# Sliding-window attention with a gated feed-forward on one core: inverse softmax sums spread by TensorE transposes of a widened copy, applied one step later

## The chip, the cores and the metric

One core of one Trainium2 chip. The metric is the device time of one execution in microseconds. Each engine works through a queue of its own in order: TensorE (PE, its weight loads shown apart as PEld), VectorE (DVE), ScalarE (ACT), GpSimd (POOL) and the queue that issues most DMAs (SP). An instruction that waits at the head of a queue holds everything behind it.

## What is computed

The reference, cut to what matters:

```python
# attention: B=4, H=8, S=768, D=64, 8 global keys, 96 local keys
scores = (q @ k.T) / 8 + bias          # bias = -slope(head) * distance
scores = where(keep, scores, -1e9)     # keep: key is global, or 0 <= q - k < 96
a = exp(scores - max(scores))
a = a / (sum(a) + 1e-9)                # the inverse sums: one number for each query and head
x = a @ v                              # -> [B, S, 512]
# feed-forward, 512 -> 1024 -> 512
h = relu(x @ w_in)
c = conv over 3 neighbouring positions of h, weights conv_w
out = (h * sigmoid(c)) @ w_out
```

The weights of the feed-forward come as float64 and are decoded on the chip.

## The kernel before, in words

**Work units.** A *job* m is one batch, one half of the sequence (384 queries) and one pair of heads: 32 jobs. A job has three *steps* i = 0, 1, 2 of 128 queries, so there are 96 steps s = 3m + i. Four jobs make one *unit* n, whose 384 positions then go through the feed-forward: 8 units.

**One step.** `scores` (L373) multiplies 128 queries with 232 keys for both heads on TensorE; `maxima` (L408) adds the bias and takes the row extremum on VectorE; `exps` (L425) takes the exponential on ScalarE, whose accumulator gives the row sums, into `sums[m]`. Two steps later (`LAG_T`) `transposes` (L454) turns the exponentials on TensorE into the PSUM tile `t`, four transposes a step, and ScalarE copies them to `pt` (L464, L465, L467).

**One job's end.** `inverses(m)` (L436) takes the reciprocals of the 6 sums of each query row on VectorE, [128 queries, 6]. They are needed the other way round: `pv[m]`, the product with v, has head dimension on partitions (64 for each of two heads) and 384 queries along the row, so that each query's inverse must stand on all 64 partitions of its head. Before, `spread(m)` (L441) transposes [128, 6] to [6, 128] on TensorE (L443), copies that to `row` on ScalarE (L445), and issues six DMAs on SP (L449), each of which repeats one row of 128 numbers over 64 partitions of `rs[m]`. `values(m)` (L470) multiplies v with `pt` into `pv[m]` on TensorE (24 matmuls, L475), and at its end multiplies `pv[m]` with `rs[m]` on VectorE (L486), rounds the product to `xh` on ScalarE (L487) and takes the rest `xl` on GpSimd (L488). `xh` and `xl` are the input of the feed-forward. `spread(m-1)` stands in step (m, 1) and `values(m-1)` in step (m, 2).

**The feed-forward.** `mm1` (L495) forms h with three passes over the four jobs' `xh`, `xl` (L506), `relu` moves it to `hbuf` (L519 on ScalarE, L517 on VectorE), `conv` is one instruction on GpSimd (L555) and two on VectorE (L556, L557), `gate` and `saturated` are on ScalarE (L575, L586), `split` on VectorE, ScalarE and GpSimd (L607 to L610), `mm2` on TensorE (L619). These items stand in a queue, and `fill(k)` puts some of them between the attention's instructions of each step, `k` being what is left divided by `left`, the steps still to go in the unit.

**What sets the order.** In the first 11 steps (`HAND`) the order on all engines is that of the code. From then on only TensorE's order is that of the code; a scheduler orders the other engines by its own model of time. In the first steps TensorE also runs idle multiplications (`warm`, L163). The first five jobs (`NATIVE`) multiply q and k as they are loaded (L389), later ones after a split by `prep` (L134 to L145) into `qh`, `ql`, `kk` (L399). The weights' decoding (L318, L320, L322 on VectorE, L327 on ScalarE, L334 on GpSimd) is put into the steps piece by piece, 16 pieces of 512 KB (loads on SP, L305).

**PSUM.** There are eight banks: three for scores (`ps_s`), one for transposes (`ps_t`), one for `pv` (`ps_v`; the transposed sums stand in the same bank), three for the feed-forward (`ps_m`). A native step takes two banks of `ps_s`, a later step one.

## Time and profile before

| | |
|---|---|
| three runs | 563.7, 564.24, 567.82 us; median 564.24 us |
| the profiled execution's own time | 566.89 us |
| its span, first to last instruction | 565.1 us |
| mean granted TensorE clock | 0.914 of full speed |
| VectorE, ScalarE, GpSimd busy | 373.5, 303.9, 257.9 us |
| DMA | 68.10 MB, mean 121 GB/s |
| rs<-row | 192 DMAs of 32 KB, median 4.6 us from issue to landing |

Lines named L... are those of the kernel before. In a list of waits the columns are the waiting engine and line, the releaser, the total in us, the number of times and the longest. In a timeline they are start, duration in us, engine, line, instruction, and in brackets the engine's idle time before it with its releaser. In a row of one line's instructions, the three numbers behind the count are the shortest, median and longest duration in ns.

The execution has five stretches that the text refers to: set-up and the first steps (0 to 23 us), the rest of the native steps (23 to 73 us), steps in which most of the weights are decoded beside the first unit (73 to 125 us), the regular steps (125 to 500 us), and the end (500 to 565 us), where the last unit's feed-forward runs and the weights are read once more for a check of their range.

### The profile page before, as it was taken

To read this page: it belongs to the slowest core of one execution; us is meant where nothing else is said; L and a number is where in the kernel's file an instruction comes from. 1 tells how busy PE (TensorE), PEld (TensorE's weight loads), DVE (VectorE), ACT (ScalarE), POOL (GpSimd) and SP (SyncE) were. 2 spreads that over 40 slices of the span, in tenths; PEclk is the share of its full clock that TensorE was granted. 3 is DMA by queue.
4 is the path that set the end of the run, shared out by engine and by line. 5 is a ranking of instruction groups with operands and counts; after the bars stand their busy time and mean duration, and the time that the engine had idled before them with its cause. 6 is when DMAs were issued, how large, how long until landed. Compare 5 with 4: busy or idle time off the path is not lost.

```text
span 565.1 us, 9158 instructions
## 1 busy us (share of the span) xinstructions
PE 474.3 (84%) x3045; PEld 405.1 (72%) x3045; DVE 373.5 (66%) x825; ACT 303.9 (54%) x825; POOL 257.9 (46%) x210
## 2 busy tenths in 40 slices
PE   7686686676967899998978899899978899988795
PEld 6464465575965689787867798788867788777584
DVE  5346599996796758754867788557669677137720
ACT  2345475665756556652565646644655487246710
POOL 4023477663873745673554355574534442233000
PEclk8957688887997979998998899999979899999999
DMA  6844876645553644465555654475545534476511
GB/s 193 200 93 106 186 216 181 139 125 127 101 115 22 149 89 96 115 139 117 107 107 108 143 90 81 78 169 127 109 55 129 118 44 78 82 209 197 179 57 43
DMA packets 38328, 68.10 MB, mean 121 GB/s; under 512 B 6145, under 2 KB 19969, under 8 KB 38273
## 3 DMA queue, kind: packets, MB, share of 16 engines
q1 hardware_dynamic: 34816, 61.28, 50.5%
q10 hardware_dynamic: 3456, 6.16, 2.9%
q8 instruction: 26, 0.43, 0.3%
q14 instruction: 30, 0.24, 0.1%
HBM read 54.84 MB, written 6.29 MB: 108 GB/s over the span
## 4 chain that ended last, share of the span: by engine, by line
DMA 22%; DVE 22%; PE 22%; SPq 12%; ACT 11%; issue 8%; POOL 2%; DVEq 0%; ACTq 0%; POOLq 0%
DMA rs<-row 15%; SPq L449 11%; PE h L506 9%; PE o L619 7%; DVE c L557 3%; DMA check<-in_w_in 3%; DVE c L556 3%; ACT pbuf L430 3%; DVE s L418 3%; DVE c L607 2%; DMA check<-in_w_out 2%; DVE rs L486 2%; DVE w L320 2%; ACT sat L586 1%; PE s L399 1%
## 5 line engine op out<-in xcount | busy, mean ns | idle before, releaser
L430 ACT ACTIVATE pbuf<-s,mm 128x232 f32<-128x232 f32 (+1 forms) x192 | 82.1, 433 | 68.5 <-DVE mm L418 66.7
L555 POOL TENSOR_SCALAR c<-hbuf,cw 128x382 f32<-128x382 f32 (+1 forms) x64 | 47.7, 748 | 78.7 <-ACT hbuf L519 41.4
L619 PE MATMUL o<-woh,gh 128*128 128x512 f32 x192 | 82.5, 430 | 0.8 <-ACT hbuf L519 0.7
L418 DVE CUSTOM_DVE_ANT_0 s<-s,tab 128x232 f32<-128x232 f32 (+1 forms) x192 | 73.0, 385 | 15.2 <-PE s L399 8.2
L619 PE MATMUL o<-woh,gl 128*128 128x512 f32 x192 | 78.4, 408 | 2.9 <-DVE gl L610 2.9
L619 PE MATMUL o<-wol,gh 128*128 128x512 f32 x192 | 78.4, 408 | 0.0
L506 PE MATMUL h<-xh,wih 128*128 128x384 f32 x252 | 60.3, 358 | 18.6 <-ACT xh L487 15.0
L460 PE MATMUL t<-ident,pbuf 128*128 128x128 f32 (+1 forms) x192 | 55.6, 311 | 23.7 <-ACT pt L467 17.2
L488 POOL TENSOR_TENSOR xl<-rs,xh 128x384 fp32r<-128x384 f32 x32 | 37.8, 1180 | 81.0 <-ACT xh L487 74.8
L145 POOL TENSOR_TENSOR ql<-rq,qh 128x768 fp32r<-128x768 f32 x24 | 48.3, 2011 | 44.3 <-DVE qh L140 23.8
L143 POOL TENSOR_TENSOR kk<-rk,kk 64x1008 fp32r<-64x1008 f32 (+1 forms) x27 | 61.0, 2260 | 11.8 <-POOL ql L145 4.5
L556 DVE SCALAR_TENSOR_TENSOR c<-hbuf,cw,c 128x382 f32<-128x382 f32 (+1 forms) x64 | 52.0, 815 | 19.6 <-POOL c L555 19.3
L506 PE MATMUL h<-xl,wih 128*128 128x384 f32 x252 | 62.0, 370 | 0.2 <-POOL xl L488 0.2
L506 PEld LDWEIGHTS h<-xh,wih 128*128 128x128 f32 x252 | 45.9, 199 | 22.1 <-ACT xh L487 17.1
L506 PE MATMUL h<-xh,wil 128*128 128x384 f32 x252 | 61.4, 369 | 0.0
L467 ACT ACTIVATE pt<-t 128x512 f32<-128x512 f32 x80 | 47.1, 589 | 22.0 <-PE t L461 22.0
L475 PE MATMUL pv<-pt,v 104*64 104x128 f32 (+2 forms) x768 | 55.1, 289 | 2.4 <-ACT row L445 1.5
L557 DVE SCALAR_TENSOR_TENSOR c<-hbuf,cw,c 128x382 f32<-128x382 f32 (+1 forms) x64 | 54.9, 858 | 0.8
L460 PEld LDWEIGHTS t<-ident,pbuf 128*128 128x128 f32 (+1 forms) x192 | 27.7, 144 | 38.5 <-ACT pt L467 21.3
L475 PEld LDWEIGHTS pv<-pt,v 104*64 104x64 f32 (+2 forms) x768 | 43.4, 141 | 15.1 <-issue 6.2
L486 DVE TENSOR_TENSOR rs<-pv,rs 128x384 f32<-128x384 f32 x32 | 17.7, 553 | 54.6 <-DMA rs<-row 50.8
L461 PE MATMUL t<-ident,pbuf 128*128 128x128 f32 x192 | 53.2, 299 | 0.0
(112 smaller groups left out, 990.4 us busy)
## 6 DMA issues: line engine op xcount, KB each, us to landing
v<-in_vv SPq DMA_DIRECT2D x32, 384.0 KB, 4.2
rq<-in_qk SPq DMA_DIRECT2D x27, 384.0 KB, 4.0
rk<-in_qk SPq DMA_DIRECT2D x15, 504.0 KB, 3.6
rs<-row SPq DMA_DIRECT2D x192, 32.0 KB, 4.6
out<-ob ACTq DMA_DIRECT2D x23, 256.0 KB, 2.1
rk<-in_qk SPq DMA_DIRECT2D x12, 408.0 KB, 3.8
wr<-in_w_in SPq DMA_DIRECT2D x8, 512.0 KB, 5.5
wr<-in_w_out SPq DMA_DIRECT2D x8, 512.0 KB, 4.4
```

Source lines behind the costliest of these rows:

```text
L143: G.tensor_tensor(kk[64:], rk[64:], kk[64:].bitcast(F32), ALU.subtract)
L145: X.tensor_tensor(ql, rq, qh.bitcast(F32), ALU.subtract)
L418: last_ttr[s] = V.tensor_tensor_reduce(out=sp[j][:, c0 : c0 + n], in0=sp[j][:, c0 : c0 + n], in1=tb, scale=-0.125, scalar=3.0e38, op0=ALU. ...
L430: last_exp[s] = A.activation(pb[:, j, c0 : c0 + n], sp[j][:, c0 : c0 + n], AF.Exp, bias=mm[:, j : j + 1], scale=-1.0, accum_out=sums[m][:, ...
L449: nc.sync.dma_start(rs[m][64 * j : 64 * j + 64, i * P : (i + 1) * P], row[c : c + 1].unsqueeze(1).broadcast_to([1, D, P]),)
L460: T.transpose(pt[:ka, j, 0, :], pb[:, j, c0:P], ident)
L461: T.transpose(pt[:, j, 1, :], pb[:, j, P:256], ident)
L475: T.matmul(pv[m][64 * j : 64 * j + 64, i * P : (i + 1) * P], vt[m][:n, i, c, 64 * j : 64 * j + 64], sb[:n, j, c, :], start=c == 0, stop=c ...
L506: T.matmul(ps[:, :TB], w_[:, k, fs], x_, start=part == 0 and k == 0, stop=part == 2 and k == NK - 1,)
L556: V.scalar_tensor_tensor(c, *tap(0), c, ALU.mult, ALU.add)
L557: V.scalar_tensor_tensor(c, *tap(2), c, ALU.mult, ALU.add)
L619: T.matmul(ps, g_[:, f], w_[:, f], start=f == 0 and part == 0, stop=f == NF - 1 and part == 2,)
```

## The change

The six DMAs, the transposition to [6, 128] and the copy to `row` are gone. Instead `spread(m)` widens the inverses on GpSimd: each of a query's 6 numbers is repeated 64 times, giving `wide`, [128, 3 x 128]. It now stands directly behind `inverses(m)`, in step (m+1, 0). A new function `turned(m)`, directly behind `values(m)`, transposes the three 128 x 128 blocks of `wide` on TensorE into a bank of `ps_t`, and ScalarE copies the 384 columns to `rs[m]`. The product with `pv`, `xh` and `xl` become a function of their own, `mixed(m)`, one step after `values(m)`; since the feed-forward's input is complete a step later, a unit's queue is spread over one step more (`left`).

With the sums' transposition gone from it, `pv[m]` is allocated in `values`. `ps_s` has two banks and `ps_t` two; native steps take their second head's scores from `ps_m`. `sums` is laid out by step and head. `load_v(m)` is issued in step (m, 0), behind the values of job m-2 that free its buffer, instead of a step earlier; the native loads go one job further ahead (job 2 gets buffers of its own and is loaded in step 1). `rs` and `wide` have one buffer each, where `rs` had two.

```diff
-    ps_s = pool("ps_s", 3, space=PSUM)
-    ps_t = pool("ps_t", 1, space=PSUM)
+    ps_s = pool("ps_s", 2, space=PSUM)
+    ps_t = pool("ps_t", 2, space=PSUM)
...
-            rk = p2.tile([P, w // 2], F32, tag="kk", name=f"rk{m}")
-            rq = p2.tile([P, TB], F32, tag="qh", name=f"rq{m}")
+            rk = (p1 if m == 2 else p2).tile([P, w // 2], F32, tag="rk" if m == 2 else "kk", name=f"rk{m}")
+            rq = p2.tile([P, TB], F32, tag="ql" if m == 2 else "qh", name=f"rq{m}")
...
-            sp = [ps_s.tile([P, 256], F32, tag="s", name=f"s{s}_{j}") for j in range(2)]
+            other = ps_m.tile([P, 512], F32, tag="m", name=f"s{s}_1")
+            sp = [ps_s.tile([P, 256], F32, tag="s", name=f"s{s}_0"), other]
...
     def spread(m):
-        pv[m] = ps_v.tile([P, TB + P], F32, tag="v", name=f"pv{m}")
-        T.transpose(pv[m][: 2 * NB, TB:], sums.pop(m)[:, 2], ident)
-        row = p1.tile([2 * NB, P], F32, tag="row", name=f"row{m}")
-        A.activation(row, pv[m][: 2 * NB, TB:], AF.Copy)
-        rs[m] = p2.tile([P, TB], F32, tag="rs", name=f"rs{m}")
-        for c in range(2 * NB):
-            j, i = divmod(c, NB)
-            nc.sync.dma_start(
-                rs[m][64 * j : 64 * j + 64, i * P : (i + 1) * P],
-                row[c : c + 1].unsqueeze(1).broadcast_to([1, D, P]),
-            )
+        inv = sums.pop(m)[:, 2]
+        wide = p2.tile([P, NB, 2, D], F32, tag="wide", name=f"wide{m}", bufs=1)
+        G.tensor_copy(wide, inv.unsqueeze(3).broadcast_to([P, NB, 2, D]))
+        wides[m] = wide.rearrange("p i j d -> p i (j d)")
+
+    def turned(m):
+        wide = wides.pop(m)
+        pt = ps_t.tile([P, 2, 2, P], F32, tag="t", name=f"rt{m}")
+        flat = pt.rearrange("p j c q -> p (j c q)")[:, :TB]
+        for i in range(NB):
+            T.transpose(flat[:, i * P : (i + 1) * P], wide[:, i], ident)
+        rs[m] = p2.tile([P, TB], F32, tag="rs", name=f"rs{m}", bufs=1)
+        A.activation(rs[m], flat, AF.Copy)
...
     def values(m):
+        pv[m] = ps_v.tile([P, TB], F32, tag="v", name=f"pv{m}")
...
+    def mixed(m):
         xh = px.tile([P, TB], F32R, tag="xh", name=f"xh{m}")
...
             if ends(s - LAG_V):
                 values((s - LAG_V) // NB)
+                turned((s - LAG_V) // NB)
             if s >= LAG_T:
                 transposes(s - LAG_T)
             maxima(s)
             exps(s)
+            if ends(s - LAG_V - 1):
+                mixed((s - LAG_V - 1) // NB)
             if i == 0 and m:
                 inverses(m - 1)
-            elif i == 1 and m:
                 spread(m - 1)
...
-                left = SPU - (e + 1) % SPU
+                left = SPU - (e + 1) % SPU + 1
                 if e + 1 >= len(steps) - SPU:
-                    left += 2
+                    left += 1
...
+            if ends(e):
+                mixed(e // NB)
             if s <= len(steps) and i < 1:
                 inverses((s - 1) // NB)
-            elif s == len(steps) + 1 or i == 1:
-                spread(s // NB - 1)
+                spread((s - 1) // NB)
...
+        elif s == 1:
+            load(2)
...
-            if 1 <= m < NATIVE - 1:
-                load(m + 1)
+            if 1 <= m < NATIVE - 2:
+                load(m + 2)
...
-        if s >= 2 and (s - 2 - (LAG_V - 3)) % NB == 0:
-            load_v((s - 2 - (LAG_V - 3)) // NB + 1)
+        if s >= NB and i == 0:
+            load_v(m)
```

**VectorE at the first job's end, before.** L486 is job 0's product; the first ISA rows behind it are step 5's maxima, then come a limit check and a weight piece's decoding (`w`).

```order
L322 SCALAR_TENSOR_TENSOR w_0_284<-wr_0_214,w_0_284 128x512
L486 TENSOR_TENSOR rs_353<-pv_349,rs_353 128x384
L418 ISA s_0_382,mm_411<-s_0_382,tab 128x232
L418 ISA mm_411 128x1
L418 ISA s_1_383,mm_411<-s_1_383,tab 128x232
L418 ISA mm_411 128x1
L236 TENSOR_SCALAR misc<-num 128x1
```

The same place in the changed kernel, where the product is L492:

```order
L322 SCALAR_TENSOR_TENSOR w_0_290<-wr_0_214,w_0_290 128x512
L419 ISA s_0_380,mm_410<-s_0_380,tab 128x232
...
L318 TENSOR_SCALAR w_0_429<-wr_0_252 128x512
L320 SCALAR_TENSOR_TENSOR w_0_429<-wr_0_252,w_0_429 128x512
L419 ISA s_0_433,mm_443<-s_0_433,tab 128x136
L419 ISA mm_443 128x1
L419 ISA s_1_432,mm_443<-s_1_432,tab 128x136
L419 ISA mm_443 128x1
L492 TENSOR_TENSOR rs_400<-pv_383,rs_400 128x384
```

The product has moved behind the maxima of steps 5 and 6 and two decoding instructions of the next weight piece.

**TensorE at the start of a unit's feed-forward (unit 3, steps 51 and 52), before.** `o` is the previous unit's second product, `s` the scores of step 51, `h_0` the first block of the new unit; `xh_2617` is the input that the last job gives.

```order
L619 MATMUL o_5_2563<-wol,gh_5_1980 128x512
L619 MATMUL o_5_2563<-woh,gl_5_1981 128x512
L399 MATMUL s_2644<-kk_2537,qh_2535 128x136
L399 MATMUL s_2644<-kk_2537,ql_2536 128x136
L399 MATMUL s_2644<-kk_2537,qh_2535 128x136
L399 MATMUL s_2644<-kk_2537,ql_2536 128x136
L506 MATMUL h_0_2657<-xh_2137,wih 128x384
L506 MATMUL h_0_2657<-xh_2316,wih 128x384
L506 MATMUL h_0_2657<-xh_2480,wih 128x384
L506 MATMUL h_0_2657<-xh_2617,wih 128x384
```

In the changed kernel (`xh_2601` is the last job's; the first `s` row is step 51's, the second step 52's; what is left out holds four transposes and ten further `o` rows):

```order
L400 MATMUL s_2590<-kk_2492,ql_2491 128x136
L625 MATMUL o_5_2545<-woh,gh_5_1978 128x512
...
L625 MATMUL o_5_2545<-woh,gl_5_1979 128x512
L400 MATMUL s_2641<-kk_2492,qh_2490 128x232
...
L512 MATMUL h_0_2651<-xh_2129,wih 128x384
L512 MATMUL h_0_2651<-xh_2309,wih 128x384
L512 MATMUL h_0_2651<-xh_2461,wih 128x384
L512 MATMUL h_0_2651<-xh_2601,wih 128x384
```

Twelve matmuls of the unit before, four transposes and step 52's scores now stand between step 51's scores and the first use of the last job's `xh`.

More of the change, by code (lines that the diff above doesn't have):

```diff
@@ L370, in fast_path @@
     last_ttr = {}
-    st_s, st_pt, pv, xt, sums, rs, line = {}, {}, {}, {}, {}, {}, {}
+    st_s, st_pt, pv, xt, sums, rs, wides = {}, {}, {}, {}, {}, {}, {}
     def scores(s):
@@ L413, in maxima @@
         if i == 0:
-            sums[m] = p1.tile([P, 3, 2 * NB], F32, tag="sums", name=f"sums{m}", bufs=3)
+            sums[m] = p1.tile([P, 3, NB, 2], F32, tag="sums", name=f"sums{m}", bufs=3)
         for j in range(2):
@@ L431, in exps @@
                 pb[:, j, c0 : c0 + n], sp[j][:, c0 : c0 + n], AF.Exp,
-                bias=mm[:, j : j + 1], scale=-1.0, accum_out=sums[m][:, 0, NB * j + i : NB * j + i + 1],
+                bias=mm[:, j : j + 1], scale=-1.0, accum_out=sums[m][:, 0, i, j : j + 1],
             )
@@ L485, in values @@
         x = rs.pop(m)
-        V.tensor_tensor(x, pv[m][:, :TB], x, ALU.mult)
+        V.tensor_tensor(x, pv[m], x, ALU.mult)
         cur["mixed"] = A.activation(xh, x, AF.Copy)
@@ L811, in fast_path @@
                 values((s - LAG_V) // NB)
+                turned((s - LAG_V) // NB)
             if s < len(steps) + LAG_T:
```

## Prediction

> **What bounds the kernel now.** First the page, for shares and the chain that ended last:
>
> ```profile
> span 565.1 us, 9158 instructions
> PE 474.3 (84%) x3045; PEld 405.1 (72%) x3045; DVE 373.5 (66%) x825; ACT 303.9 (54%) x825; POOL 257.9 (46%) x210
> DMA 22%; DVE 22%; PE 22%; SPq 12%; ACT 11%; issue 8%; POOL 2%; DVEq 0%; ACTq 0%; POOLq 0%
> ```
>
> No engine is full. TensorE is nearest, and a third of the chain is DMAs and the queue that issues them. What binds differs by stretch, so next the busy time by window:
>
> ```profile
> core 0: us, PE busy (x) PEld busy (x) DVE busy (x) ACT busy (x) POOL busy (x), PEclk, DMA share, GB/s
> 0.00:23.00 23.00, 18.86 (x178) 15.11 (x178) 12.23 (x45) 8.36 (x28) 7.09 (x30) 0.93 0.72 206
> 23.00:73.00 50.00, 32.70 (x179) 23.02 (x179) 26.62 (x74) 20.85 (x67) 16.49 (x14) 0.69 0.62 133
> 73.00:125.00 52.00, 36.94 (x241) 33.27 (x242) 51.00 (x92) 33.66 (x87) 37.08 (x25) 0.87 0.63 166
> 125.00:500.00 375.00, 334.35 (x2223) 291.76 (x2222) 255.05 (x547) 214.82 (x586) 191.23 (x134) 0.94 0.52 104
> 500.00:565.00 65.00, 51.49 (x229) 41.90 (x227) 28.57 (x67) 26.21 (x59) 6.02 (x8) 0.96 0.44 137
> ```
>
> From 23 to 73 us nothing is full: something waits. From 73 to 125 us VectorE is (51.0 of 52). From 125 to 500 us TensorE works 334.35 of 375 us; it stands 40.65 us. So the third view is the waits: VectorE's in the first 125 us and TensorE's from 125 to 500 us, the largest of each.
>
> ```profile
> DVE rs L486 <- DMA rs<-row: 22.9, 5, 9.0
> ...
> PE h L506 <- ACT xh L487: 15.0, 7, 3.4
> PE t L460 <- ACT pt L467: 10.7, 7, 3.4
> PE pv L443 <- DVE sums L439: 8.1, 1, 8.1
> PE t L460 <- ACT pt L465: 6.3, 5, 1.6
> ```
>
> The first row is VectorE standing for the spread inverses. The next four add up to 40.1 us, nearly all that TensorE stands in the regular steps. How one wait spreads shows in the timeline at 44 us, one row each of VectorE, ScalarE and TensorE:
>
> ```profile
> 44.40 0.56 DVE L486 TENSOR_TENSOR rs<-pv,rs 128x384 f32<-128x384 f32 x1 [9.02 <-DMA rs<-row]
> ...
> 44.99 0.52 ACT L487 ACTIVATE xh<-rs 128x384 fp32r<-128x384 f32 x1 [7.94 <-DVE rs L486]
> ...
> 46.52 0.82 PE L389 MATMUL s<-rk,rq 64*128 64x136 f32 x2 [4.65 <-ACT pbuf L430]
> ```
>
> The product stands at the head of VectorE's queue for 9.02 us with the next maxima behind it; ScalarE stands 7.94 us, and TensorE waits for exponentials that waited for those maxima.
>
> **The change, part by part. Product behind the DMAs, 0 to 125 us.** The DMAs go, and the product moves a step back, behind two steps' maxima; its `rs` then comes from TensorE and ScalarE. At most the 22.9 us vanish. But from 23 to 73 us 50 x 133 = 6650 KB of loads must still come, at the 206 GB/s of the first stretch 32 us, so no more than 18 of the 50 us can go (VectorE's 26.62 us of work allow more). I hold that at least one longest stall, 9 us, goes. The value taken is 16, nearer the upper end since loads have nothing of the DMA's waits ahead of them on SP any more. The native steps' other edits (second head's scores in another pool, earlier loads, `load_v` later) serve these same steps and are counted in the 16.
>
> **Widening on GpSimd.** 32 copies of 128x384, not seen before. The nearest rows are the one-input instruction of about that size and the two-input one of exactly that size; behind them two VectorE lines, 32-bit decoding and the cast of `kk`:
>
> ```profile
> L555 POOL TENSOR_SCALAR c<-hbuf,cw x64: 584/594/1409, 80.2 to 524.7; 128x382 f32<-128x382 f32 x32, 128x386 f32<-128x386 f32 x32
> L488 POOL TENSOR_TENSOR xl<-rs,xh x32: 995/1017/2002, 28.8 to 494.8; 128x384 fp32r<-128x384 f32 x32
> ...
> L320 DVE SCALAR_TENSOR_TENSOR w<-wr,w x16: 651/693/2848, 12.7 to 113.9; 128x512 int32<-128x512 int32 x16
> ...
> L136 DVE CAST kk<-rk x19: 656/2264/2420, 180.5 to 449.9; 128x1008 fp32r<-128x1008 f32 x11, 128x816 fp32r<-128x816 f32 x8
> ```
>
> I take 0.59 us a copy (bounds 0.58 and 1.02), 19 us in all, which fits into GpSimd's idle half; were that cover gone, all 19 us would show. But equal VectorE instructions differ fourfold, the median cast 2.26 us against 0.66 at best: they seem to be held up while GpSimd works. Where VectorE is full, 73 to 125 us, some five copies fall: between 0 and 5 x 0.59 = 3 us. I take +1, the middle being 1.5 and a copy often meeting an instruction that is not held.
>
> The Trainium skill speaks against the change here ("SBUF — State Buffer", section "SBUF: two separate sides"): GpSimd and VectorE share a pair of ports under an exclusive lock, held for a whole instruction, and a GpSimd instruction that reads SBUF blocks a VectorE one with two SBUF inputs. The two VectorE rows above agree with it. By that rule the full 3 us would be lost in that stretch, and the sum would stand 2 us higher.
>
> **Transposes on TensorE.** Three a job in place of one; their pace and the small one's are seen at 290 and 292 us:
>
> ```profile
> 290.27 0.27 PE L461 MATMUL t<-ident,pbuf 128*128 128x128 f32 x1
> 290.37 0.27 PE L460 MATMUL t<-ident,pbuf 128*128 128x128 f32 x1
> 290.48 0.27 PE L461 MATMUL t<-ident,pbuf 128*128 128x128 f32 x1
> ...
> 292.31 0.27 PE L399 MATMUL s<-kk,ql 128*128 128x232 f32 x1
> 292.42 0.27 PE L443 MATMUL pv<-ident,sums 128*6 128x128 f32 x1
> 296.09 0.33 PE L460 MATMUL t<-ident,pbuf 128*128 128x128 f32 x1 [3.40 <-ACT pt L467]
> ...
> 298.14 0.63 PE L619 MATMUL o<-woh,gl 128*128 128x512 f32 x1
> 298.56 0.63 PE L619 MATMUL o<-woh,gh 128*128 128x512 f32 x1
> 298.99 0.63 PE L619 MATMUL o<-wol,gh 128*128 128x512 f32 x1
> ```
>
> One starts 0.11 us after another, the small one 0.11 after its forerunner. From 125 us on 24 jobs end: 24 x 3 x 0.11 = 7.9 us come, 24 x 0.11 = 2.6 go. TensorE is the fullest engine there, so the whole +5.3 counts (bounds 0, if they lie in its waits, and 7.9).
>
> **ScalarE.** A copy of 384 columns out of PSUM (the row of `hbuf`, of that size and source) in place of `row`:
>
> ```profile
> L519 ACT ACTIVATE hbuf<-h x50: 462/488/507, 77.8 to 524.2; 128x384 f32<-128x384 f32 x50
> ...
> L445 ACT ACTIVATE row<-pv x32: 248/250/267, 19.3 to 485.4; 6x128 f32<-6x128 f32 x32
> ```
>
> 24 x (0.488 - 0.250) = 5.7 us more beside 214.82 of 375: hidden under TensorE's work, at worst 5.7.
>
> **TensorE's waits, 125 to 500 us.** Of the 8.1 us for VectorE's reciprocals I count 5: TensorE meets the widened sums one step later, behind `values`, and the 375 us hold some 70 steps of 5 us. The 15.0 for `xh` should go too: as the order rows show, twelve matmuls, four transposes and four scores now lie between, and the product no longer waits for a DMA. Of the 17.0 for `pt` I count half, 8: with two banks two transposes in a row are free, but `turned` takes one of them, so that the transposes behind `values` still need the eviction of the step before, and the next ones that of `rs`. That is 28. A part comes back as waits for whatever is then late: VectorE's 255.05 us in a shorter stretch, ScalarE's in-order queue. I take four fifths, 22 (bounds 10, the reciprocals' 5 and a third of the `xh` waits, and 40).
>
> The clock is a second gain. Behind the 3.40 us gap above, `o` matmuls start 0.43 us apart; 291 us shows the usual pace:
>
> ```profile
> 291.29 0.39 PE L619 MATMUL o<-woh,gh 128*128 128x512 f32 x1
> 291.52 0.39 PE L619 MATMUL o<-wol,gh 128*128 128x512 f32 x1
> 291.75 0.40 PE L619 MATMUL o<-woh,gl 128*128 128x512 f32 x1
> ```
>
> 0.23 apart, so that some six matmuls lose 0.2 us each, over 1 us a gap of this length. The granted clock of this stretch is 0.94, worth at most 0.06 x 375 = 22 us. I take 4 (bounds 0 and 10).
>
> **The end**, 500 to 565 us, has neither removed nor added waits of TensorE that bear on it: 0.
>
> **Sum** against the profiled execution's own 566.89 us: -16 + 1 + 5.3 - 22 - 4 = -35.7, that is 531.2. That execution stood 2.65 us over the median of the runs, 564.24; so **528 us**.
>
> **The rivals.**
>
> *The head alone gains.* What ends TensorE's waits in the regular steps is replaced: `pt`, `rs` and `xh` share ScalarE's queue, whose order the scheduler changes. For it speaks that `pt` waits are ScalarE's lateness, not a lack of work; against it that ScalarE was late, as at 44.99 us, behind an `xh` whose product waited for the DMA. 566.9 - 16 + 1 + 5.3 = 557.2, less 2.65: 554.5.
>
> *More goes than I count.* All 18 us in the head, all 40 of TensorE's waits, 10 of clock: 566.9 - 18 - 40 - 10 + 5.3 - 2.65 = 501.5. Against it: VectorE would work 255 us in some 320, with bursts that are full.
>
> *Two score banks are too few (slower).* Now `scores(s)` needs the exponentials of s-2 done, where it needed those of s-3. Two places, ScalarE's last row of a step, then TensorE's first row two steps later:
>
> ```profile
> 311.50 0.20 ACT L430 ACTIVATION_READ_ACCUMULATOR pbuf<-s,mm 128x1 f32 x1
> ...
> 312.81 0.27 PE L399 MATMUL s<-kk,qh 128*128 128x232 f32 x1
> ...
> 164.55 0.27 PE L399 MATMUL s<-kk,qh 128*128 128x232 f32 x1
> ...
> 168.05 0.20 ACT L430 ACTIVATION_READ_ACCUMULATOR pbuf<-s,mm 128x1 f32 x1
> ```
>
> In the first, steps 60 and 62, 1.1 us are left over, the tightest I found after 200 us. In the second, steps 32 and 34, the scores start 3.7 us before those exponentials end: with two banks they would wait. It decides from 35.7 / 81 = 0.44 us of new wait in each of the 81 later steps; at 0.8 us it gives 528 + 65 = 593.
>
> *VectorE waits on as long, for ScalarE's copy instead of the DMA.* The change then doesn't do what it says: the stalls of the head and the 15.0 for `xh` stay, the reciprocals' 5 and half of `pt` go, at four fifths 10, with 2 of clock: 566.9 + 1 + 5.3 - 10 - 2 - 2.65 = 558.5; if the clock's 2 and the 10 come back behind the later products, 570: about 564. Against it: copy and product lie a step apart.
>
> **How the numbers follow.** Forecast 0.55, head alone 0.17, more 0.13, banks 0.07, the copy late 0.08. About 1% (5.6 us) is what a measurement of this kernel can tell from no change. Faster by more: forecast, more, and 0.12 of the head alone (under 558.6 in seven tenths of its spread): 0.80. Within: 0.05 of the head alone and the copy late: 0.13. Slower: 0.07. The range 500 to 557 leaves out the banks, the copy late and a part of the most favourable case, 0.2 together; its ends are near the two outer cases, 501.5 and 554.5, which the bounds of the costs also reach.
>
> **What would show it.** Right: no VectorE wait of the product over 1 us; the first 73 us shorter by 12 to 18; TensorE's idle time in the regular steps under 25 us, with no row for `sums` or `xh` above 2 us; copies on GpSimd near 0.6 us. Wrong: a row of scores waiting for exponentials (`s` <- `pbuf`) above 10 us after the native steps; `t` <- `pt` as large as before; VectorE waiting for ScalarE's copy; the stretch of full VectorE longer than 52 us; or a native stretch held by loads.

## The result, and the profile after

The changed kernel takes **525.07 us** (median of 4 runs, 524.25 to 525.77) against 565.33 for the kernel before on the same chip: ratio 0.928, 95% interval 0.924 to 0.933. The forecast was 528, with a range of 500 to 557. The profiled execution took 525.77 us, 524.0 of it span. One execution of f1, an experiment below, fell in a slower state (581.6 us, granted clock 0.73) and is left out of its median.

From the page of the changed kernel, the span, the busy shares and the chain that ended last:

```profile
span 524.0 us, 8851 instructions
...
PE 463.0 (88%) x3109; PEld 400.2 (76%) x3109; DVE 384.8 (73%) x825; ACT 311.5 (59%) x825; POOL 278.1 (53%) x242
...
DVE 35%; PE 35%; ACT 9%; POOL 7%; DMA 6%; issue 5%; SPq 1%; POOLq 0%; ACTq 0%; DVEq 0%
```

DMAs and the queue that issues them held 34% of the chain; they hold 7% now, and VectorE and TensorE hold 70% where they held 44%.

To compare kernels of different length, the span is cut at the same work: the first scores of step 15 (the end of the native steps, "head" below), of step 26 (the end of the stretch with VectorE full) and of step 95. Busy time by window, cut so, before:

```profile
core 0: us, PE busy (x) PEld busy (x) DVE busy (x) ACT busy (x) POOL busy (x), PEclk, DMA share, GB/s
0.00:70.30 70.30, 49.35 (x349) 36.52 (x350) 36.49 (x115) 27.78 (x92) 22.51 (x43) 0.77 0.65 156
70.30:125.40 55.10, 39.55 (x252) 35.28 (x251) 53.35 (x97) 35.49 (x91) 38.32 (x27) 0.86 0.64 166
125.40:475.50 350.10, 309.45 (x2069) 271.18 (x2069) 247.54 (x533) 203.74 (x563) 182.46 (x129) 0.94 0.52 105
475.50:565.10 89.60, 75.99 (x380) 62.07 (x378) 36.08 (x82) 36.90 (x82) 14.63 (x13) 0.97 0.47 124
```

and after, with the same columns:

```profile
0.00:44.70 44.70, 40.17 (x358) 30.49 (x358) 33.39 (x111) 27.75 (x88) 24.67 (x47) 0.92 0.77 234
44.70:102.70 58.00, 38.65 (x255) 34.83 (x253) 55.66 (x100) 37.39 (x94) 43.15 (x31) 0.85 0.46 153
102.70:435.80 333.10, 307.41 (x2118) 271.55 (x2117) 260.31 (x536) 208.41 (x561) 195.19 (x152) 0.97 0.31 95
435.80:524.00 88.20, 76.73 (x385) 63.34 (x383) 35.47 (x82) 37.98 (x83) 15.04 (x14) 0.95 0.39 121
```

The second number of a row is the length of the stretch: head -25.6, full stretch +2.9, regular steps -17.0, the last -1.4, together the 41.1 us by which the spans differ. In the head TensorE has 358 matmul records where it had 349, yet is busy 9.2 us less: its granted clock is 0.92 instead of 0.77. In the regular steps it stands 333.10 - 307.41 = 25.7 us where it stood 40.65.

What became of the stall, one product of the head in the timeline (start, duration, engine), with VectorE's maxima ahead of it and ScalarE's `xh` behind:

```profile
28.49 0.31 DVE L419 CUSTOM_DVE_ANT_0 s<-s,tab 128x136 f32<-128x136 f32 x1 [0.21 <-POOL tab L218]
...
28.72 0.55 DVE L492 TENSOR_TENSOR rs<-pv,rs 128x384 f32<-128x384 f32 x1
...
29.30 0.52 ACT L493 ACTIVATE xh<-rs 128x384 fp32r<-128x384 f32 x1
```

The product has no bracket: it waited for nothing, where one of before stood 9.02 us. Over the whole run VectorE's products wait six times, none of them in the head, and 9.6 of the 13.8 us are one wait near the end:

```profile
DVE rs L492 <- ACT rs L455: 13.8, 6, 9.6
```

TensorE's largest waits in the regular steps after:

```profile
PE t L463 <- ACT rs L455: 11.0, 7, 2.5
PE h L512 <- ACT xh L493: 8.1, 5, 2.9
PE s L400 <- ACT pbuf L431: 4.1, 2, 2.9
PE h L512 <- POOL xl L494: 2.2, 3, 1.0
```

The rows for `sums` and `pt` are gone, the one for `xh` is halved, and a new one stands first: the transposes wait for the bank from which ScalarE still has to copy the turned inverses. The `xl` row (0.2 us before) belongs beside the one for `xh`: both are the input that the unit's last job gives, and together they are 10.3 us.

### The profile page after: what moved, and what is told of

Its sections match the earlier page's. It is cut to its first block, busy times and chain, and to the rows that moved or that the text cites. A ratio compares the mean times of both kernels' runs of the same rounds, so it can differ in the third digit from the quotient of the medians.

```text
span 524.0 us, 8851 instructions
## 1 busy us (share of the span) xinstructions
PE 463.0 (88%) x3109; PEld 400.2 (76%) x3109; DVE 384.8 (73%) x825; ACT 311.5 (59%) x825; POOL 278.1 (53%) x242
## 4 chain that ended last, share of the span: by engine, by line
DVE 35%; PE 35%; ACT 9%; POOL 7%; DMA 6%; issue 5%; SPq 1%; POOLq 0%; ACTq 0%; DVEq 0%
PE o L625 15%; PE h L512 8%; DVE c L562 7%; DVE c L563 6%; DVE s L419 5%; DVE kk L136 4%; PE s L400 3%; DMA check<-in_w_out 3%; DVE c L613 3%; PE pv L479 3%; DMA check<-in_w_in 2%; PE t L463 2%; ACT pbuf L431 2%; PE t L464 2%; DVE qh L140 2%
## 5 line engine op out<-in xcount | busy, mean ns | idle before, releaser
L143 POOL TENSOR_TENSOR kk<-rk,kk 64x1008 fp32r<-64x1008 f32 (+1 forms) x27 | 65.9, 2439 | 16.2 <-PE pv L479 5.1
L562 DVE SCALAR_TENSOR_TENSOR c<-hbuf,cw,c 128x382 f32<-128x382 f32 (+1 forms) x64 | 59.2, 929 | 18.3 <-POOL c L561 17.9
L512 PE MATMUL h<-xh,wih 128*128 128x384 f32 x252 | 58.5, 351 | 9.1 <-ACT xh L493 8.1
L463 PE MATMUL t<-ident,pbuf 128*128 128x128 f32 (+1 forms) x192 | 51.3, 292 | 17.2 <-ACT rs L455 17.1
L563 DVE SCALAR_TENSOR_TENSOR c<-hbuf,cw,c 128x382 f32<-128x382 f32 (+1 forms) x64 | 62.2, 975 | 0.8
L512 PE MATMUL h<-xl,wih 128*128 128x384 f32 x252 | 58.3, 352 | 2.2 <-POOL xl L494 2.2
L512 PE MATMUL h<-xh,wil 128*128 128x384 f32 x252 | 57.8, 353 | 0.0
L616 POOL TENSOR_TENSOR gl<-c,gh 128x1024 fp32r<-128x1024 f32 (+2 forms) x16 | 36.5, 2287 | 35.2 <-ACT gh L614 35.1
L400 PE MATMUL s<-kk,qh 128*128 128x232 f32 (+1 forms) x162 | 41.9, 281 | 11.5 <-ACT pbuf L431 11.5
L464 PE MATMUL t<-ident,pbuf 128*128 128x128 f32 x192 | 50.3, 287 | 0.2 <-POOL pbuf L282 0.2
L613 DVE SCALAR_TENSOR_TENSOR c<-c,hbuf 128x1024 f32<-128x1024 f32 (+2 forms) x28 | 43.9, 1593 | 7.6 <-ACT sat L592 7.6
```

The costliest lines, as they stand in the source:

```text
L143: G.tensor_tensor(kk[64:], rk[64:], kk[64:].bitcast(F32), ALU.subtract)
L400: last_mm[s] = T.matmul(sp[j][:, c0 : c0 + n], q_[:, j * TB + i * P : j * TB + (i + 1) * P], kk[:, j * w + k0 : j * w + k0 + n], start=st, ...
L463: T.transpose(pt[:ka, j, 0, :], pb[:, j, c0:P], ident)
L464: T.transpose(pt[:, j, 1, :], pb[:, j, P:256], ident)
L512: T.matmul(ps[:, :TB], w_[:, k, fs], x_, start=part == 0 and k == 0, stop=part == 2 and k == NK - 1,)
L562: V.scalar_tensor_tensor(c, *tap(0), c, ALU.mult, ALU.add)
```

## The experiments

Twelve kernels, each timed beside the kernel before. The columns in the middle are the stretches of the profiled execution, cut as above; "idle" is what TensorE stands in the regular steps (stretch less its busy time, from the same windows). One profiled execution each, so stretches a few us apart are not told apart.

| kernel | us, median | ratio to before, 95% | head | full | regular | idle | last |
|---|---|---|---|---|---|---|---|
| before | 565.3 | 1 | 70.3 | 55.1 | 350.1 | 40.7 | 89.6 |
| changed | 525.1 | 0.924 to 0.933 | 44.7 | 58.0 | 333.1 | 25.7 | 88.2 |
| e1, DMAs, product a step later | 540.7 | 0.953 to 0.965 | 62.6 | 55.3 | 328.3 | 23.0 | 90.2 |
| f1, e1 with the old deal | 548.1 | 0.965 to 0.979 | 62.2 | 58.4 | 337.5 | 31.9 | 91.1 |
| e2, same step, old deal | 526.1 | 0.927 to 0.938 | 46.5 | 58.6 | 329.6 | 22.9 | 87.5 |
| e8, old deal | 523.5 | 0.917 to 0.932 | 44.1 | 59.1 | 332.1 | 23.2 | 88.1 |
| e4, loads as before | 528.0 | 0.931 to 0.938 | 48.7 | 56.7 | 332.0 | 26.1 | 88.7 |
| e5, banks alone | 558.7 | 0.985 to 0.992 | 69.4 | 54.0 | 341.8 | 34.0 | 91.5 |
| t1, transposes alone | 546.4 | 0.964 to 0.975 | 58.2 | 56.4 | 345.4 | 33.6 | 88.0 |
| e6, copy twice | 524.2 | 0.920 to 0.934 | 47.2 | 53.2 | 333.0 | 25.5 | 88.6 |
| e9, eviction on VectorE | 535.7 | 0.940 to 0.953 | 44.0 | 56.5 | 346.9 | 36.0 | 87.8 |
| h1, transposes at both ends | 523.7 | 0.919 to 0.933 | 45.3 | 55.2 | 334.0 | 28.9 | 87.4 |
| i1, inverses in matmul pool | 520.6 | 0.919 to 0.930 | 45.6 | 57.0 | 329.1 | 23.6 | 87.6 |
| i3, i1 with the old deal | 524.8 | 0.924 to 0.932 | 45.1 | 55.4 | 335.9 | 24.7 | 89.3 |

**The theory**: VectorE's stall behind the DMAs is the cause, in the head directly and in the regular steps through late `xh`; the transposes remove it, and the second bank removes the `pt` waits. **Rivals**: the later place of the product did it, or the longer deal, the loads, or the banks.

### e1: the DMAs back, all else changed

```diff
 def spread(m):
-    G.tensor_copy(wide, inv.unsqueeze(3).broadcast_to([P, NB, 2, D]))
+    T.transpose(pv[m][: 2 * NB, TB:], sums.pop(m)[:, 2], ident)
+    A.activation(row, pv[m][: 2 * NB, TB:], AF.Copy)
+    for c in range(2 * NB):
+        nc.sync.dma_start(rs[m][...], row[c : c + 1]...)
...
             if i == 0 and m:
                 inverses(m - 1)
+            elif i == 1 and m:
                 spread(m - 1)
```

> The changed kernel (525.1 us), but the inverse sums are spread as before: small transpose, row, six DMAs, at the second step of the next job; the product stays a step later, banks and loads stay as changed. Theory, the DMA itself is what VectorE stands for, and it lasts longer than the step that the product was put back: VectorE's waits rs<-DMA stay at 5 to 12 us of the 22.9 of before, nearly all ahead of 60 us, where steps last 3 us and the loads share the DMA engines; in the regular steps, of 4 to 5 us, they are gone, TensorE has 5.3 us of transposes less and no t<-rs wait. Together 523 to 532 us, step 15's scores 5 to 10 us later than at 44.7 us. Rival, the placement alone did it: no rs<-DMA row above 1 us, step 15's scores at 45 us or earlier, and 515 to 521 us since the transposes are saved.

540.7 us: slower than both expected, and 15.6 over the changed kernel. VectorE's whole wait for the DMAs, then one spread, with SP's issue of the six:

```profile
DVE rs L492 <- DMA rs<-row: 46.0, 13, 8.3
```

```profile
238.22 0.25 ACT L446 ACTIVATE row<-pv 6x128 f32<-6x128 f32 x1
...
238.49 3.88 SPq L450 DMA_DIRECT2D rs<-row  x6
...
246.95 0.56 DVE L492 TENSOR_TENSOR rs<-pv,rs 128x384 f32<-128x384 f32 x1 [5.35 <-DMA rs<-row]
```

The product begins 8.5 us after `row`: SP takes 3.88 us to issue six DMAs, and they land 4 us and more behind. One step is less than 5 us, so a step's delay doesn't cover it, and I was wrong to expect that the wait would vanish in the regular steps: 23.2 of the 46.0 us lie there. Yet those steps take 328.3 us, no longer than with transposes. What costs is the head, 62.6 us against 44.7. VectorE still stands 13.1 us for the DMAs up to 70 us (22.2 before). So the later place alone did not do it; replacing the DMAs is worth 17.9 us there. One thing besides the DMAs is back in e1: the spread stands in the second step of the next job, as before, and not directly behind the reciprocals. DMAs issued that one step earlier were not run, so how much of the 17.9 us they would have saved stays open.

### e2: the product in the same step, with the old deal

```diff
                 turned((s - LAG_V) // NB)
+                mixed((s - LAG_V) // NB)
...
-                left = SPU - (e + 1) % SPU + 1
+                left = SPU - (e + 1) % SPU
...
-            if ends(e):
-                mixed(e // NB)
```

> The changed kernel, but the product follows the turned inverses in the same step, at the head of VectorE's queue as before, and a unit's work is dealt over the steps as before. Theory, both parts are needed: the transposes take the DMA's time out of the head, but in the regular steps the product stands for ScalarE's copy, which comes late in its queue; VectorE's rs<-rs waits rise from 13.8 (9.6 of it at the very end) to 25 us or more, TensorE's xh waits come back to 12 to 18 us from 8.1 in the regular steps: 531 to 542 us, the first 44.7 us longer by 0 to 3. Rival, only the DMA mattered: 522 to 528 us and the xh waits stay at 6 to 10.

526.1 us: the rival's number, not mine. VectorE's products wait 17.6 us for the copied inverses, not 25 or more, and in the regular steps `xh` and `xl` together cost TensorE about what they cost in the changed kernel (10.7 us and 10.3):

```profile
PE t L463 <- ACT rs L455: 7.7, 5, 3.0
PE h L512 <- POOL xl L494: 5.5, 3, 2.1
PE h L512 <- ACT xh L493: 5.2, 3, 3.7
```

Once the inverses come by transposes, the later step is worth nothing measurable.

### e8 and f1: the deal, with transposes and with DMAs

The same edit, e8 in the changed kernel, f1 in e1:

```diff
-                left = SPU - (e + 1) % SPU + 1
+                left = SPU - (e + 1) % SPU
                 if e + 1 >= len(steps) - SPU:
-                    left += 1
+                    left += 2
```

> The changed kernel, but with a unit's work dealt over the steps as before (left = 12 - (e + 1) % 12, two more in the last unit). Theory, the xh waits fell because the longer deal leaves matmuls of the last unit to do first: without it the first h matmul meets the product of its own step, TensorE's xh waits in the regular steps rise from 8.1 to 14 us or more, and the whole takes 530 to 538 us. Rival, they fell because VectorE no longer stands for the DMA when the product comes up: xh waits of 6 to 11 us, and 523 to 528 us.

> The kernel with the DMA spread and the product a step later (540.7 us), but with a unit's work dealt over the steps as before. Theory, in the regular steps there the product still stands for DMAs (32.4 us of waits), and only the longer deal keeps that from TensorE by leaving it matmuls of the last unit: without it the xh waits rise from 3.4 to 10 us or more, step 26 to 95 from 328.3 to 336 or more, the whole to 546 to 556 us. Rival, the step that the product was put back is enough: xh waits up to 7 us, 537 to 544 us.

e8: 523.5 us, again the rival; `xh` is 5.5 us and `xl` 5.5, together 11.0 against the changed kernel's 10.3. f1: 548.1 us, as my theory had it, 7.4 over e1, with

```profile
PE h L512 <- ACT xh L493: 14.3, 7, 3.3
```

where e1 had

```profile
PE h L512 <- ACT xh L493: 3.4, 4, 1.4
```

`xl` adds 2.2 us in f1 and 3.2 in e1. The two parts are substitutes: with DMAs the longer deal takes these waits from 16.5 to 6.6 us, with transposes only from 11.0 to 10.3. A late product harms TensorE only if the unit's first matmuls come right behind it: either it isn't late (transposes), or there are other matmuls to do first (the longer deal).

### e4: the loads as before

```diff
-        elif s == 1:
-            load(2)
...
-            if 1 <= m < NATIVE - 2:
-                load(m + 2)
+            if 1 <= m < NATIVE - 1:
+                load(m + 1)
...
-        if s >= NB and i == 0:
-            load_v(m)
+        if s >= 2 and (s - 2 - (LAG_V - 3)) % NB == 0:
+            load_v((s - 2 - (LAG_V - 3)) // NB + 1)
```

> The changed kernel, with the loads of q, k and v of the native jobs issued when and where they were before. Theory, in the head what is left without the DMA stall is the loads: job 2's and later q and k, issued a job later, are what native steps then wait for, so that step 15's scores come 4 to 12 us later than at 44.7 and the whole takes 529 to 537 us; the load rate of the head falls from 234 GB/s towards 200. Rival, the loads are hidden behind the decoding and the maxima: step 15's scores within 2 us of 44.7, 523 to 527 us.

528.0 us, between the two expected; step 15's scores come at 48.7, the near end of the theory's 4 to 12 us. The whole is 2.9 us over the changed kernel, but the intervals of the ratios overlap, so that a price for the loads is likely and not shown.

### e5 and t1: one part alone, on the kernel before

```diff
-    ps_s = pool("ps_s", 3, space=PSUM)
-    ps_t = pool("ps_t", 1, space=PSUM)
+    ps_s = pool("ps_s", 2, space=PSUM)
+    ps_t = pool("ps_t", 2, space=PSUM)
```

with the native second head in `ps_m`, is all of e5. t1 has before's banks, loads and deal, but:

```diff
-    T.transpose(pv[m][: 2 * NB, TB:], sums.pop(m)[:, 2], ident)
...
+    G.tensor_copy(wide, inv.unsqueeze(3).broadcast_to([P, NB, 2, D]))
...
+    flat = ps_m.tile([P, 512], F32, tag="m", name=f"rt{m}")[:, :TB]
+    for i in range(NB):
+        T.transpose(flat[:, i * P : (i + 1) * P], wide[:, i], ident)
+    A.activation(rs[m], flat, AF.Copy)
```

> The kernel before (565.3 us) with only the banks changed: two for scores and two for transposes, the native steps' second head in the pool of the matmuls. Theory, the second bank is worth about half of TensorE's 17.0 us of waits t<-pt in the regular steps, the DMA stalls and the xh waits stay: 555 to 561 us, t<-pt under 6 us there, rs<-DMA at 20 us or more. Rival, the banks are worth nothing by themselves, since another result of ScalarE is then waited for, s<-pbuf above 8 us: 563 to 568 us.

> The kernel before with the DMA spread alone replaced: widened copy, three transposes and ScalarE's copy, product in the same step as before; three banks for scores, one for transposes, loads and deal as before. The turned inverses lie in the pool of the matmuls (ps_m), since they can't share the one bank of the transposes. Theory, the parts add up: the same-step kernel with new banks and loads took 526.1 us, the banks alone were worth 6.6 on the kernel before, the loads 2.9 on the changed one, so 532 to 539 us, with the head (step 15's scores) at 48 to 52 us and t<-pt waits of 12 us or more left. Rival, the transposes gain in the head only, and the regular steps need the second bank for them: head at 48 to 52 us, but step 26 to 95 as long as before, 346 to 352 us, and 543 to 550 us in all.

e5: 558.7 us, 1.2% less than before, as the theory had it: no `t`<-`pt` row of any size is left, the regular steps are 8.3 us shorter, and the `xh` waits stay (17.1). t1: 546.4 us, the rival's number, but only in part by the rival's way. Its regular steps, 345.4, stay long, as the rival had them; the one bank costs more than the 17.0 us of before:

```profile
PE t L461 <- ACT pt L468: 10.3, 8, 2.4
PE t L461 <- ACT pt L466: 10.2, 5, 3.3
```

Its head, 58.2 us, neither expected. Three windows of it:

```profile
22.00:32.00 10.00, 8.38 (x49) 5.55 (x48) 7.35 (x26) 5.87 (x20) 4.60 (x6) 0.75 0.54 154
32.00:42.00 10.00, 9.29 (x49) 6.93 (x46) 4.80 (x17) 4.22 (x14) 4.22 (x4) 0.50 0.44 122
42.00:50.00 8.00, 8.00 (x46) 5.66 (x44) 4.22 (x12) 3.98 (x13) 2.04 (x3) 0.50 0.75 242
```

From 32 to 50 us TensorE's clock stands at 0.50, it is busy nearly throughout, and VectorE is half idle: here TensorE holds the head. VectorE's product, in the same step as the transposes, stands for ScalarE's copy, and that copy for the transposes (12 to 58 us):

```profile
DVE rs L490 <- ACT rs L453: 9.8, 3, 5.3
...
ACT rs L453 <- PE rt L451: 9.1, 3, 4.1
```

That is the prediction's rival of the late copy, in this kernel's head. The parts don't add: against the kernel before timed beside each, some 17.5 us (t1) and 6.6 (e5) alone, but 39.2 together with the loads (e2).

### e6: GpSimd's copy issued twice

```diff
         G.tensor_copy(wide, inv.unsqueeze(3).broadcast_to([P, NB, 2, D]))
+        G.tensor_copy(wide, inv.unsqueeze(3).broadcast_to([P, NB, 2, D]))
```

> The changed kernel with GpSimd's widening copy issued twice into the same buffer: 32 more copies of 0.50 us. Theory, where VectorE is full (step 15's scores to step 26's) a copy on GpSimd costs VectorE its whole length, since the two hold each other up: that stretch was 55.1 us before and is 58.0, 56.7 and 58.6 us in the three kernels with one copy a job, 55.3 in the one without copies; with two it takes 60 to 61.5 us, and the whole 527 to 531 us. Rival, GpSimd's idle half takes the copy, and the 2.9 us have another cause: the stretch stays at 57 to 59 us and the whole at 523 to 527 us.

524.2 us in all, the rival's number. With 32 more copies of 0.50 us the full stretch is even the shortest of all:

```profile
47.20:100.40 53.20, 37.49 (x253) 34.63 (x251) 52.75 (x89) 35.43 (x88) 46.42 (x34) 0.83 0.51 164
```

and step 26 comes at 100.4 us, not later than the changed kernel's 102.7. GpSimd's idle half takes the copies, and the trace shows how. Seven copies begin in this stretch. Six of them last 0.70 to 0.95 us, and each of the six began while a two-input VectorE instruction (`w` L320 or `c` L563) was already running, such as:

```profile
86.42 0.96 DVE L320 SCALAR_TENSOR_TENSOR w<-wr,w 128x512 int32<-128x512 int32 x1
...
86.79 0.95 POOL L446 COPY wide<-sums 128x384 f32<-128x384 f32 x1
```

There the copy got longer and GpSimd, not VectorE, paid. So the 2.9 us are not the copies' price. By the windows they come and go with how much decoding the head leaves over: VectorE's busy time up to step 26 is 89.8 us before, 89.1 after and 90.7 here.

### e9: VectorE copies the turned inverses

```diff
-        A.activation(rs[m], flat, AF.Copy)
+        V.tensor_copy(rs[m], flat)
```

> The changed kernel, but VectorE instead of ScalarE copies the turned inverses out of PSUM. Theory, what is left of the waits for the transposes' banks (t<-rs 17.1 us) is ScalarE's crowded queue: with VectorE, busy 73% of the span, they fall under 8 us, and the whole takes 519 to 523 us although the full stretch gains some 2 us. Rival, VectorE is no nearer: the copy comes behind a whole step's maxima there, the waits stay at 13 us or more, and the whole takes 525 to 530 us.

535.7 us: worse than either expected. In the regular steps:

```profile
PE h L512 <- ACT xh L493: 20.2, 5, 5.2
PE t L463 <- DVE rs L455: 8.5, 5, 3.0
```

```profile
209.76 0.54 DVE L455 COPY rs<-rt 128x384 f32<-128x384 f32 x1
...
210.34 0.56 DVE L492 TENSOR_TENSOR rs<-pv,rs 128x384 f32<-128x384 f32 x1
```

In this pair the copy comes only right ahead of the product, behind VectorE's other work of the step, and both are late: what was a bank's wait became a wait for `xh`.

### h1: transposes for the first five and the last four jobs only

```diff
+TURN = lambda m: m < NATIVE or m >= 28
...
 def spread(m):
+    if not TURN(m):
+...
+        return
```

> Transposes for the first five jobs and the last four, DMAs (with the product a step later) for the 23 between. From the stretches of the runs so far: with DMAs throughout, step 15 to 26 takes 55.3 us against 58.0 in the changed kernel, and step 26 to 95 takes 328.3 against 333.1, while the head takes 62.6 against 44.7. Theory, the stretches are independent, since from step 15 on VectorE's stalls for the DMA hold up nothing that TensorE needs, while the transposes are work on the fullest engine: 44.7 + 55.3 + 328.3 + 88.2 = 516.5 us of span, 518.3 us in all, within 515 to 521. Rival, the regular steps of the DMA kernel were short only because work was put off out of its longer head: 523 to 527 us, step 26 to 95 above 331 us.

523.7 us, the rival's number. The head is as short as with transposes throughout, but step 26 to 95, where all jobs but the last four have DMAs, takes 334.0 us, not e1's 328.3. That is what it takes with transposes (333.1): after the head, with the product a step later and the longer deal, replacing the DMAs gains nothing that these runs show. e1's gain in the regular steps does not come without its longer head, so no price for the transposes can be read from that pair.

### i1 and i3: the turned inverses in the pool of the matmuls

```diff
-        pt = ps_t.tile([P, 2, 2, P], F32, tag="t", name=f"rt{m}")
-        flat = pt.rearrange("p j c q -> p (j c q)")[:, :TB]
+        flat = ps_m.tile([P, 512], F32, tag="m", name=f"rt{m}")[:, :TB]
```

i3 has the old deal besides.

> The changed kernel, but the turned inverses lie in one of the three banks of the matmuls instead of one of the two of the transposes. Theory, the 17.1 us of t<-rs waits come from the bank that the turned inverses hold until ScalarE copies them: they go, at four fifths, and the whole takes 509 to 516 us, with no new wait of h or o for rs above 4 us. Rival, TensorE waits just as long for another late result of ScalarE, since its queue is no shorter (t<-pt, s<-pbuf or h<-rs rise by 10 us or more): 521 to 528 us.

> The changed kernel with two edits that took it to 520.6 and 523.5 us one by one: turned inverses in the pool of the matmuls, and a unit's work dealt over the steps as before. Theory, with the transposes in place the deal no longer matters, since the product stands for nothing: 518 to 523 us, step 26 to 95 within 3 us of the 329.1 of the kernel with the first edit, xh waits no larger than its 9.0. Rival, the longer deal is what covers the product's extra step once the t<-rs waits are gone: xh waits of 14 us or more and 526 to 532 us.

i1: 520.6 us, the fastest of all, 4.4 us below the changed kernel, though the intervals of their ratios overlap (0.919 to 0.930, 0.924 to 0.933). That is just under the rival's range and short of the theory's. In the regular steps the 11.0 for `rs` are gone, and most of them are back under other names:

```profile
PE h L511 <- ACT xh L492: 9.0, 4, 3.1
PE s L400 <- ACT pbuf L431: 4.9, 3, 3.7
PE pv L478 <- ACT pt L469: 4.8, 4, 1.4
PE t L462 <- ACT pt L467: 2.5, 2, 1.2
```

i3: 524.8 us over 7 runs, between what the two expected: `xh` 8.4 as the theory had it, but 5.5 for `xl` besides, and regular steps of 335.9 us, 6.8 over i1's where the theory allowed 3. ScalarE's queue is the common source of nearly all these rows; a bank only decides which of its results is waited for.

## Why the prediction was right, step by step

**Product behind the DMAs: -16 counted, -25.6 measured.** The mechanism held; the term was mis-sized by its cap of 18 us, taken from the 206 GB/s of the first 23 us. That rate was no limit:

```profile
12.00:22.00 10.00, 9.64 (x106) 7.50 (x103) 8.72 (x38) 6.91 (x26) 3.59 (x5) 1.00 1.04 307
22.00:32.00 10.00, 9.60 (x86) 7.03 (x86) 9.23 (x26) 7.69 (x26) 8.03 (x9) 1.00 0.82 251
```

are windows of the changed kernel, 307 and 251 GB/s. At 300 GB/s the forecast's 6650 KB of loads need 22 us, not 32. Nor did the term count the clock: the head's 0.77 became 0.92, and TensorE's busy time there fell by 9.2 us. Taken back from the changed kernel one by one, the DMAs cost the head 17.9 us (e1), the old loads 4.0 (e4) and the product's old place 1.8 (e2). Kernels with the same loads, transposes and later product have heads of 44.0 to 47.2 us, so the last two are hardly told from chance, and as the parts don't add, the 25.6 can't be split among them.

**Widening on GpSimd: +1 counted for the full stretch.** The copies took 0.50 us, not 0.59, and e6 shows no price for more of them in this stretch. The stretch is 2.9 us longer, but, by VectorE's busy times, as work put off from the head. By the rule of the Trainium skill that the prediction weighed ("SBUF — State Buffer", section "SBUF: two separate sides") the four copies that begin there would, as an estimate, cost up to 2.0 us, and e6's seven, 5.5 us long in all, up to 5.5. That is not what e6 measured: six of the seven met a VectorE instruction that had begun first, and there the copy was held up. Elsewhere VectorE did get busier: in the regular steps 260.31 us where it was 247.54, with 536 instructions for 533. e6's further copies did not raise that (259.44), so its cause stays open. Of the two VectorE rows that the prediction named for the rule, only the one of `w` has two inputs; the cast has one and was held up all the same (last section).

**Transposes +5.3 and clock -4 in the regular steps.** TensorE's busy time went from 309.45 to 307.41 us with 49 more matmul records: -2.0 for the two terms together, against +1.3 counted. The clock rose from 0.94 to 0.97.

**TensorE's waits: -22 counted, -15.0 measured** (40.65 to 25.7 idle). The reciprocals' row went whole, 8.1 where I counted 5, and `pt` whole, 17.0 where I counted 8. `xh`, all of whose 15.0 I counted as gone, kept 8.1, and 11.0 of `t`<-`rs` came new. I had named this eviction as what later transposes would need, and gave back too little for it: a fifth of 28 is 6, and 11.0 + 4.1 + 2.0 came, for `rs`, `pbuf` and `xl`. The reason for `xh` was half wrong: I argued from the twelve matmuls and four transposes that the order puts between. e8 takes the deal back, and `xh` and `xl` together hardly rise (11.0 against 10.3); it is the missing DMA that brings them down from 15.2. f1 shows that the order would have mattered had the DMAs stayed.

**The end: 0 counted, -1.4 measured.** One product waits 9.6 us for ScalarE there, and nothing that TensorE needs comes late by it.

The errors of size are opposite: the head 9.6 us better than counted, the full stretch 1.9 worse, the regular steps 3.7 less (-17.0 against -20.7), the end 1.4 better. That 528 met 525 owes something to that, and so to luck. The comparison by parts is rough besides, since the forecast cut by time (73, 125 and 500 us) and the table by steps (70.3, 125.4 and 475.5 us before). Of the rivals, "more goes than I count" held in the head alone. Two score banks cost less than it took to decide: 4.1 us of `s`<-`pbuf` in the regular steps and 7.3 in the full stretch, where 35.7 would have undone the gain.

**The signs I had named.** No product's wait over 1 us: right in the head and the full stretch, not later (six in all, above). The waits in the regular steps were up to 1.5 us, the one near the end 9.6. First stretch shorter by 12 to 18: it was 25.6. Idle under 25: 25.7. No `xh` row above 2: it was 8.1. Two signs of being wrong came. One is a row of scores waiting for exponentials above 10 us after the native steps:

```profile
PE s L400 <- ACT pbuf L431: 11.5, 5, 3.4
```

No such row stood before, and with the banks changed alone (e5) it is 7.5 us: it comes with the bank taken from the scores, for which the sum had no term of its own. The other is the full stretch longer than 52 us (58.0), my sign of the port's price. Its reading was wrong, and its measure too: cut at the same work that stretch was 55.1 us already before.

## What to carry to other kernels

A small DMA in a chain of dependent steps costs its issue and its landing (here 3.9 and over 4 us for six of 32 KB), and an in-order queue passes that on to everything behind it; a transposition of a widened copy does the same in work that other engines have to spare. It paid in the head, whose steps last about 3 us; in the regular steps, with the product a step later and the longer deal, the DMAs were as good (h1). A later place and other work in between hide the same lateness, so count one of them, not both. Before capping a gain by a transfer rate, look for the highest rate in the trace, not the mean of a stretch in which the loads may not have been asked for any faster: the trace of before already had 314 GB/s from 10 to 20 us.

## What the runs showed of the hardware

**Half clock while busy.** In t1's head TensorE's granted clock stood at 0.50 from 28 to 50 us although by the profile's rows, in which the ends of matmuls are modelled, it was busy 21.3 of the 22 us; two of the eleven windows of 2 us:

```profile
30.00:32.00 2.00, 2.00 (x14) 0.50 0.96 252
...
48.00:50.00 2.00, 2.00 (x11) 0.50 0.55 164
```

The Trainium skill ("TensorE: Matmul & The Clock Gate", section "Part 1: The HAM clock gate") has the full clock return after one busy window of about 3.4 us; here some 22 us did not bring it back. These are steps 8 to 12. The changed kernel ran the scores of steps 8 to 11 at 1.00, in the windows up to 32 us above, and then had a window at 0.66 too (32 to 42 us). What sets it here stays open: most of these matmuls are scores with 64 rows, values, transposes and a few warming ones, and no run varied them alone. So it also stays open how much of t1's longer head is the banks and how much the clock.

**VectorE and GpSimd: whoever begins first.** The same 19 casts of `kk` had a median of 2.26 us before; in the changed kernel, with more work on GpSimd, the row reads

```profile
L136 DVE CAST kk<-rk x19: 581/758/2292, 152.0 to 409.4; 128x1008 fp32r<-128x1008 f32 x11, 128x816 fp32r<-128x816 f32 x8
```

0.76 us. What decides is the order of beginning. A long cast of before, and a short one of the changed kernel:

```profile
285.53 1.82 POOL L145 TENSOR_TENSOR ql<-rq,qh 128x768 fp32r<-128x768 f32 x1 [3.62 <-PE s L399]
285.62 2.26 DVE L136 CAST kk<-rk 128x1008 fp32r<-128x1008 f32 x1
```

```profile
367.65 0.68 DVE L136 CAST kk<-rk 128x1008 fp32r<-128x1008 f32 x1
367.77 2.27 POOL L145 TENSOR_TENSOR ql<-rq,qh 128x768 fp32r<-128x768 f32 x1
```

In the first GpSimd began 0.09 us sooner, and the cast ended only 0.53 us behind it. In the second the cast began 0.12 us sooner, and GpSimd's instruction took 0.45 us more. All casts in both traces follow this: the 16 long ones before and the 9 after (2.01 to 2.42 us) began while a two-input GpSimd instruction (`ql`, or `gl` of the gate) was running; the 3 and 10 short ones (0.58 to 0.76 us) began ahead of it or met none. So a price per GpSimd instruction can't be read from the work that GpSimd does in all; it depends on which of the two is running when the other comes up.
